# Weight preparation before the plain block: half-size block loads, output weights kept in place, stores on another queue, another order

## The chip, the cores and the metric

The kernel runs on one core of a Trainium2 chip. The metric is the device time of one execution in microseconds. Three executions of the kernel before took 1728.92, 1729.54 and 1729.87 us; their median is 1729.54 us.

## What is computed

Pooled attention (8 batches, 8 heads, 576 tokens, head width 64; keys and values are averaged over groups of 8) gives x of 4608 tokens by 512. Two feed-forward layers follow:

```python
h = (x @ w1) * (x @ w2) @ w3
x = h @ w_out                                  # 4608 x 512
xn = x / sqrt(mean(x * x) + 1e-6) * rms_g
g = xn @ w_gate                                # 512 -> 1536
out = (g * sigmoid(g) * (xn @ w_val)) @ w_out2 # 1536 -> 512
```

The weights come in as float64. The change touches only the weights of the second layer, w_gate, w_val and w_out2.

## The kernel before

The tokens are worked on in 9 blocks of 512. Every fp32 product is made of three matmuls (`mm3`, L86 to L89) of numbers split in a high and a low half (`split`, L82: ScalarE writes the high half, VectorE the low one). The first layer runs for blocks 0 to 8 in turn. The second layer then takes block 0 alone, by plain products (this is "the plain block", `gv` and `o_mm`), and blocks 1 to 8 in pairs, by a scheme with seven products in place of eight (`quad`, `o_part`), for which sums and differences of weight quarters are needed.

**Weight preparation.** `prep` (L807 to L815) is a list of steps that turns float64 weights into split fp32. Its unit is a `Conv` job on a 128x512 piece: `s0` loads it on SyncE's queue (L108) into one of three `raw` buffers, `s1` is one ScalarE and two VectorE instructions (L124 to L128), `s2` two more on VectorE (L133, L141), `s3` whatever comes behind it. `conv_steps(..., 2)` runs them as a pipeline: step k issues the load of job k+2, `s1` of job k, `s2` of job k-1 and `s3` of job k-2.

- `gv_jobs(G, s, kp)` is two jobs; G is 0 to 2, s is 0 for w_gate and 1 for w_val, kp a half of the rows. Behind the second, `sums` forms four more quarters (T1 to T4, L751), splits two tiles of eight quarters (L755, L756) and stores each in two DMAs of 512 KB (L763) to a DRAM scratch, `wdram[s, c, z]`, with c = 2G and 2G+1, where z = 0 holds the quarters T1, T2, B11, B12 and z = 1 holds B21, B22, T3, T4.
- `o2_jobs(g)` is four jobs for four row blocks of w_out2; behind the last, `done` splits them (ScalarE L83, VectorE L84, 128x2048) into two tiles of the pool `r` and stores these to the scratch `odram[g]` (L793, L794).

The order before is: G = 0 (8 jobs), output part 0 (4), G = 1 (8), output part 1 (4), G = 2 (8), output part 2 (4); with the pipeline's two extra steps these are 38 steps. 14 of them run during the first layer's block 7, 5 in the first half of block 8, 4 in its second half, and 15 (`rest`) in the plain block. `Ticker` spreads them: one call after each unit of matmuls, about one step a call.

**Use.** `ring_load(z, n)` (L820 to L829) loads one half of the weights of step n of the second layer from `wdram`, 1024 KB, into one of four buffers of the pool `wB`; steps n = 0 to 11 belong to the plain block. `gv` reads only the quarters B11, B12, B21 and B22 of what was loaded. `o2_load(n)` (L838 to L845) loads the two split tiles of an output part from `odram`, 1024 KB each, into the pool `wC` (four buffers, which hold the first layer's last weights `wph`, `wpl` until block 8 is done). In the plain block the loop over c = 0 to 5 runs 12 matmuls for each `gv` and each `o_mm`, with a call of `tick()` between them, and `o_mm(0, m)` uses output part m // 4 from c = 1 on.

**Queues.** All these loads and stores are issued by SyncE (SP), one behind the other; an issue whose semaphore is not there holds up all that stand behind it. The order on the queue is that of the program as the framework lowers it, which may move an issue past another whose buffer is not free yet. GpSimd (POOL) issues only the accumulating loads of k and v in attention, and computes one small power for each block's norm (L609), between two tiny transfers on SP (L605 and L610).

Of the kernel before, what the change touches and what calls it, by code (L numbers as in the profile page):

```python
# [8 lines left out]
F32 = mybir.dt.float32  # L9
# [11 lines left out]
def kernel(  # L21
# [19 lines left out]
    nc = tc.nc  # L41
# [9 lines left out]
    NB = NT // TB  # L51
    KD = DM // P
    KF1 = F1 // P
# [9 lines left out]
    wC_p = ctx.enter_context(tc.tile_pool(name="wC", bufs=4))  # L63
# [15 lines left out]
    def wtile(pool, nm):  # L79
        return pool.tile([P, 4, 512], F32R, tag="w", name=nm)  # L80
# [464 lines left out]
    for n in range(NW3):  # L545
        g, j = divmod(n, KF1)
# [116 lines left out]
    pipe = Pipe()  # L663
# [49 lines left out]
    NCH = KF2 // 2  # L713
# [8 lines left out]
    }  # L722
    odram = [dram_p.tile([2, P, 4, DM], F32, name=f"od{g}") for g in range(KF2 // 4)]
    ready = set()

    def rtile(nm, dt=F32R):
        return r_p.tile([P, 2048], dt, tag="r", name=nm)

    def gv_jobs(G, s, kp):
        cell = {}  # L730
        w = (w_gate, w_val)[s]

        def quart(z):
            if "f" not in cell:
                cell["f"] = rtile("wf", F32).rearrange("p (j f c) -> p j f c", j=2, f=8)
            f = cell["f"].bitcast(I32)
            return f[:, :, 2 + 2 * z : 4 + 2 * z, :]

        def sums(_):
            f = cell.pop("f")  # L740

            def q(n):
                return f[:, :, FI[n], :]

            for o, x, y in (
                ("T1", "B12", "B11"),
                ("T2", "B22", "T1"),
                ("T3", "B22", "B12"),
                ("T4", "B21", "T2"),
            ):  # L750
                nc.vector.tensor_tensor(out=q(o), in0=q(x), in1=q(y), op=ALU.subtract)  # L751
            for j in range(2):
                c = 2 * G + j
                st = rtile("wst").rearrange("p (f l c) -> p f l c", f=8, l=2)
                nc.scalar.copy(st[:, :, 0, :], f[:, j])  # L755
                nc.vector.tensor_tensor(  # L756
                    out=st[:, :, 1, :],
                    in0=f[:, j],
                    in1=st[:, :, 0, :].bitcast(F32),
                    op=ALU.subtract,  # L760
                )
                for z in range(2):
                    nc.sync.dma_start(  # L763
                        out=wdram[s, c, z][:, :, kp],
                        in_=st[:, 4 * z : 4 * z + 4].bitcast(F32),
                    )
                ready.add((s, c, kp))

        def view(z):
            return z.rearrange("p (j f c) -> p j f c", j=2, f=2)  # L770

        def src(z):
            k0 = (2 * z + kp) * P
            return w[k0 : k0 + P, G * 512 : (G + 1) * 512]

        return [
            Conv(src(0), raw_p, out=lambda: quart(0), view=view),
            Conv(src(1), raw_p, out=lambda: quart(1), view=view, then=sums),
        ]

    def o2_jobs(g):
        cell = {}

        def row(j):
            if j == 0:
                cell["f"] = rtile("of", F32).rearrange("p (j c) -> p j c", j=4)
            return cell["f"].bitcast(I32)[:, j, :]

        def done(_):
            f = cell.pop("f")  # L790
            hi, lo = (rtile(n).rearrange("p (j c) -> p j c", j=4) for n in ("oh", "ol"))
            split(hi, lo, f)
            nc.sync.dma_start(out=odram[g][0], in_=hi.bitcast(F32))  # L793
            nc.sync.dma_start(out=odram[g][1], in_=lo.bitcast(F32))  # L794
            ready.add(g)

        return [
            Conv(
                w_o2[(4 * g + j) * P : (4 * g + j + 1) * P, :],
                raw_p,  # L800
                out=lambda j=j: row(j),
                then=done if j == 3 else None,
            )
            for j in range(4)
        ]

    prep = []  # L807
    for G in range(3):
        part = [gv_jobs(G, s, kp) for s in range(2) for kp in range(2)]
        part = part + [o2_jobs(G)] if G == 0 else part  # L810
        if G == 2:
            part = [o2_jobs(1)] + part + [o2_jobs(2)]
        for p in part:
            prep += p
    prep = conv_steps(prep, 2)  # L815


# [1 line left out]
    ring, ring_n = {}, [0, 0]  # L819

    def ring_load(z, n):
        while ring_n[z] <= min(n, len(SEQ) - 1):
            m = ring_n[z]
            c, s = SEQ[m]
            assert (s, c, 0) in ready and (s, c, 1) in ready
            t = wB_p.tile([P, 4, 512], F32R, tag="w", name=f"wr{z}")
            ring[m, z] = t.rearrange("p f (k l c) -> p f k l c", k=2, l=2)
            nc.sync.dma_start(out=ring[m, z].bitcast(F32), in_=wdram[s, c, z])
            ring_n[z] += 1  # L829

    def wq(n, form, kp):
# [1 line left out]
        t = ring[n, f // 4]  # L833
        return t[:, f % 4, kp, 0, :], t[:, f % 4, kp, 1, :]

    o2r, o2_n = {}, [0]

    def o2_load(n):  # L838
        while o2_n[0] <= min(n, 3 * (1 + NB // 2) - 1):
            g = o2_n[0] % 3  # L840
            assert g in ready
            o2r[o2_n[0]] = [wtile(wC_p, nm) for nm in ("oh", "ol")]
            for l, t in enumerate(o2r[o2_n[0]]):
                nc.sync.dma_start(out=t.bitcast(F32), in_=odram[g][l])
            o2_n[0] += 1  # L845
# [31 lines left out]
    def xn_steps(i):  # L877
        seq = [lambda: (xn_load(i, 0), xn_load(i, 1))]
        return seq + [lambda kk=kk: xn_split(i, kk) for kk in range(KD)]
# [223 lines left out]
    def spread(steps, n):  # L1103
        return steps + [lambda: None] * (n - len(steps))

    pipe.run(NB - 2, range(KF1), ab, y_mm, Ticker(prep[:14], 3 * KF1 - 1))
    xt.pop(NB - 2)
    pipe.run(NB - 1, range(4), ab, y_mm, Ticker(prep[14:19], 12))
    ring_load(0, 1)
    ring_load(1, 1)  # L1110
    pipe.run(NB - 1, range(4, KF1), ab, y_mm, Ticker(prep[19:23] + xn_steps(0), 12))
    xt.pop(NB - 1)
    early, forms = xprep(1)
    rest = prep[23:]
    tick = Ticker(rest + early + forms, 30)
    gv(0, 0)
    gv(1, 0)
    pipe.fin()
    o2_load(0)
    for c in range(NCH):  # L1120
        if c:
            gv(2 * c, 0)
            tick()
            gv(2 * c + 1, 0)
            tick()
            ring_load(0, 2 * c + 2)
            ring_load(1, 2 * c + 2)
            o_mm(0, 2 * c - 2)
            tick()
        for f in range(2):  # L1130
            if pipe.todo:
                pipe.todo.pop(0)()
            gv(2 * c + f, 1)
            tick()
            if c and f == 0:
                o_mm(0, 2 * c - 1)
                tick()
        if c == 0:
            for st in pipe.todo:
                st()  # L1140
        ring_load(0, 2 * c + 3)
        ring_load(1, 2 * c + 3)
        if c == 1:
            o2_load(1)
        elif c == 4:
            o2_load(2)
    tick.flush()
    o_mm(0, 2 * NCH - 2)
    xn.pop(0)
# [62 lines left out]
```

## Time and profile before

| | |
|---|---|
| median of three executions | 1729.54 us |
| the profiled execution | 1729.85 us |
| its span, first to last instruction | 1728.0 us |
| TensorE busy | 1632.6 us (94%), 7252 matmuls |
| VectorE busy | 1050.2 us (61%) |
| ScalarE busy | 643.9 us (37%) |
| GpSimd busy | 59.1 us (3%) |
| mean granted TensorE clock | 0.985 |
| DMA moved | 288.95 MB, mean 167 GB/s |

Busy time of TensorE counts pipelined matmuls, so a stretch can be nearly all busy and yet hold fewer matmuls than it could; the number of matmuls in a stretch, given as (x...), says more. Times in the views are us from the span's start. The plain block lies between about 837 and 985 us.

### The profile page before, as it was taken

What the parts mean: (1) busy time and instruction counts of PE and PEld (TensorE: products, weight loads), DVE (VectorE), ACT (ScalarE), POOL (GpSimd) and SP (SyncE); (2) the same over time, 40 slices, a digit from 0 to 9 for tenths busy, and PEclk for the clock granted to TensorE, in tenths of its full rate; (3) what the DMA queues carried; (4) which work ended last, traced back from release to release, by engine and by line L of the source; (5) the groups of instructions that cost most, each with busy time, mean ns of one, the idle gap of its engine ahead of it and who ended that gap; (6) DMA issues with size and microseconds to landing.
All of it is one profiled execution on the core that took longest, in us unless ns stands there. A gap on an engine that the chain in (4) does not pass through costs nothing.

```text
span 1728.0 us, 19733 instructions
## 1 busy us (share of the span) xinstructions
PE 1632.6 (94%) x7252; PEld 1279.5 (74%) x7252; DVE 1050.2 (61%) x1885; ACT 643.9 (37%) x1568; POOL 59.1 (3%) x50
## 2 busy tenths in 40 slices
PE   6898999999999999999767999999999999999999
PEld 3566677777777777778555778888888888888887
DVE  7874574849494847878484654476255745465344
ACT  3644533333333343434332333243333234233321
POOL 0001000000100000000000000000000000000000
PEclk9999999999999999999888999999999999999999
DMA  9855232322223110588889975466454645455421
GB/s 259 213 149 104 59 70 48 60 68 40 70 38 80 26 52 1 183 292 310 305 288 406 388 280 182 160 231 244 164 202 180 248 169 218 147 196 203 184 99 74
DMA packets 144885, 288.95 MB, mean 167 GB/s; under 512 B 50954, under 2 KB 102154, under 8 KB 124820
## 3 DMA queue, kind: packets, MB, share of 16 engines
q1 hardware_dynamic: 131988, 278.23, 46.4%
q0 software_dynamic: 12800, 9.46, 4.0%
q8 instruction: 57, 0.93, 0.2%
q14 instruction: 40, 0.33, 0.1%
HBM read 237.26 MB, written 50.37 MB: 166 GB/s over the span
## 4 chain that ended last, share of the span: by engine, by line
PE 51%; issue 20%; DVE 9%; DMA 7%; ACT 2%; POOL 1%; SPq 1%; POOLq 0%; ACTq 0%
PE ps L87 9%; PE ps L88 9%; PE ps L89 9%; PE o L89 5%; PE o L88 5%; PE o L87 5%; DVE aT L329 5%; DMA kv<-in_v_dram 4%; PE y L88 2%; PE y L89 2%; PE y L87 2%; DMA wr<-wd 1%; ACT s L301 1%; PE ps L387 1%; DVE f L627 1%
## 5 line engine op out<-in xcount | busy, mean ns | idle before, releaser
L87 PE MATMUL ps<-xf,wr 128*128 128x512 f32 x576 | 227.9, 396 | 1.8 <-DVE f L1010 1.8
L88 PE MATMUL ps<-xf,wr 128*128 128x512 f32 x576 | 227.9, 396 | 0.0
L89 PE MATMUL ps<-xf,wr 128*128 128x512 f32 x576 | 227.8, 395 | 0.0
L87 PE MATMUL o<-oh,hch 128*128 128x512 f32 x384 | 149.4, 389 | 0.0
L88 PE MATMUL o<-ol,hch 128*128 128x512 f32 x384 | 149.4, 389 | 0.0
L89 PE MATMUL o<-oh,hcl 128*128 128x512 f32 x384 | 149.4, 389 | 0.0
L1006 ACT COPY f<-ps 128x512 f32<-128x512 f32 x144 | 84.4, 587 | 169.8 <-PE ps L89 165.2
L329 DVE STREAM_TRANSPOSE aT<-s 32x256 f32<-32x256 f32 x324 | 140.9, 435 | 5.5
L301 ACT ACTIVATE s<-ps,mx 128x72 f32<-128x72 f32 (+1 forms) x320 | 98.0, 322 | 106.3 <-DVE mx L298 106.3
L87 PEld LDWEIGHTS ps<-xf,wr 128*128 128x128 f32 x576 | 108.5, 188 | 27.7 <-DVE f L1010 2.2
L88 PEld LDWEIGHTS ps<-xf,wr 128*128 128x128 f32 x576 | 108.8, 189 | 25.6
L89 PEld LDWEIGHTS ps<-xf,wr 128*128 128x128 f32 x576 | 108.8, 189 | 25.5
L87 PE MATMUL y<-hh,wph 128*128 128x512 f32 x288 | 117.6, 410 | 7.2 <-DVE wpl L84 5.1
L87 PE MATMUL ps<-xh,w2h 128*128 128x512 f32 x288 | 117.9, 409 | 6.2 <-DVE f L627 3.5
L1010 DVE TENSOR_TENSOR f<-y,f 128x512 f32<-128x512 f32 x48 | 33.2, 691 | 148.5 <-PE y L89 148.5
L87 PE MATMUL ps<-xh,w1h 128*128 128x512 f32 x288 | 115.5, 401 | 2.2 <-ACT s L301 2.0
L88 PE MATMUL y<-hl,wph 128*128 128x512 f32 x288 | 114.0, 396 | 1.0 <-DVE hl L84 1.0
L89 PE MATMUL y<-hh,wpl 128*128 128x512 f32 x288 | 113.4, 394 | 0.0
L89 PE MATMUL ps<-xh,w2l 128*128 128x512 f32 x288 | 113.0, 393 | 0.0
L88 PE MATMUL ps<-xl,w2h 128*128 128x512 f32 x288 | 112.8, 392 | 0.0
L88 PE MATMUL ps<-xl,w1h 128*128 128x512 f32 x288 | 112.5, 391 | 0.0
L89 PE MATMUL ps<-xh,w1l 128*128 128x512 f32 x288 | 112.5, 390 | 0.0
(149 smaller groups left out, 3018.8 us busy)
## 6 DMA issues: line engine op xcount, KB each, us to landing
wr<-wd SPq DMA_DIRECT2D x120, 1024.0 KB
wd<-wst SPq DMA_DIRECT2D x48, 512.0 KB
raw<-in_moe_w_dram SPq DMA_DIRECT2D x32, 512.0 KB
oh<-od SPq DMA_DIRECT2D x15, 1024.0 KB
ol<-od SPq DMA_DIRECT2D x15, 1024.0 KB
raw<-in_moe_w_out_dram SPq DMA_DIRECT2D x20, 512.0 KB
ydram<-f SPq DMA_DIRECT2D x36, 256.0 KB
q<-in_q_dram SPq DMA_DIRECT2D x32, 256.0 KB
```

The lines of the kernel that those rows point to most:

```text
L87: nc.tensor.matmul(o, lh, rh, start=first, stop=False, skip_group_check=part)
L88: nc.tensor.matmul(o, lh, rl, start=False, stop=False, skip_group_check=part)
L89: nc.tensor.matmul(o, ll, rh, start=False, stop=last, skip_group_check=part)
L301: nc.scalar.activation(s_t[t][:n, h, :SP], pv[:, j, :], AF.Exp, bias=mx[:, j, :], accum_out=den_t[t][:n, h, :],)
L329: nc.vector.transpose(aT[32 * kb : 32 * kb + 32, :, s0 + 32 * i : s0 + 32 * i + 32], s_t[t][32 * i : 32 * i + 32, :, 32 * kb : 32 * kb + 32],)
L387: nc.tensor.matmul(ps[j * D : (j + 1) * D, :n], st8["vp", b][:, h * D : (h + 1) * D], st8["aT", b][:SP, h, c0 : c0 + n], start=True, stop= ...
L627: nc.vector.tensor_tensor(out=hf, in0=ps, in1=a0.pop((i, m)), op=ALU.mult)
L1006: nc.scalar.copy(t, bank)
L1010: nc.vector.tensor_tensor(out=t, in0=bank, in1=t, op=ALU.add)
```

## The change

- In the plain block `ring_load` loads only two of the four quarters of each half, 512 KB in place of 1024 KB (the two that `gv` reads). The 24 loads of steps 0 to 11 are concerned; later steps load all.
- `o2_jobs` takes its two tiles from the pool `wC` and writes the split weights straight into the tiles that `o_mm` reads. The first three `o2_load` calls (six loads of 1024 KB) are gone; the stores to `odram` remain, for the later pairs of blocks.
- The stores to `wdram` (48 of 512 KB) and to `odram` (6 of 1024 KB) are issued on GpSimd's queue in place of SyncE's.
- The order of jobs is now G = 0, G = 1, then the first job pair of G = 2, output part 0, two pairs of G = 2, output part 1, the last pair of G = 2, output part 2. 13, 4 and 4 steps run in block 7 and in the halves of block 8, 17 in the plain block. The load of block 0's activations for the plain block (`xn_load`, the first of `xn_steps(0)`) moves from the second half of block 8 to the end of its first half.

```diff
--- before.py
+++ after.py
@@ -722,6 +722,7 @@
     }
     odram = [dram_p.tile([2, P, 4, DM], F32, name=f"od{g}") for g in range(KF2 // 4)]
     ready = set()
+    o2r = {}
 
     def rtile(nm, dt=F32R):
         return r_p.tile([P, 2048], dt, tag="r", name=nm)
@@ -760,7 +761,7 @@
                     op=ALU.subtract,
                 )
                 for z in range(2):
-                    nc.sync.dma_start(
+                    nc.gpsimd.dma_start(
                         out=wdram[s, c, z][:, :, kp],
                         in_=st[:, 4 * z : 4 * z + 4].bitcast(F32),
                     )
@@ -788,11 +789,10 @@
 
         def done(_):
             f = cell.pop("f")
-            hi, lo = (rtile(n).rearrange("p (j c) -> p j c", j=4) for n in ("oh", "ol"))
+            hi, lo = o2r[g] = [wtile(wC_p, nm) for nm in ("oh", "ol")]
             split(hi, lo, f)
-            nc.sync.dma_start(out=odram[g][0], in_=hi.bitcast(F32))
-            nc.sync.dma_start(out=odram[g][1], in_=lo.bitcast(F32))
-            ready.add(g)
+            nc.gpsimd.dma_start(out=odram[g][0], in_=hi.bitcast(F32))
+            nc.gpsimd.dma_start(out=odram[g][1], in_=lo.bitcast(F32))
 
         return [
             Conv(
@@ -806,12 +806,12 @@
 
     prep = []
     for G in range(3):
-        part = [gv_jobs(G, s, kp) for s in range(2) for kp in range(2)]
-        part = part + [o2_jobs(G)] if G == 0 else part
-        if G == 2:
-            part = [o2_jobs(1)] + part + [o2_jobs(2)]
-        for p in part:
-            prep += p
+        for s in range(2):
+            for kp in range(2):
+                if (G, kp) == (2, 1):
+                    prep += o2_jobs(s)
+                prep += gv_jobs(G, s, kp)
+    prep += o2_jobs(2)
     prep = conv_steps(prep, 2)
 
 
@@ -825,7 +825,10 @@
             assert (s, c, 0) in ready and (s, c, 1) in ready
             t = wB_p.tile([P, 4, 512], F32R, tag="w", name=f"wr{z}")
             ring[m, z] = t.rearrange("p f (k l c) -> p f k l c", k=2, l=2)
-            nc.sync.dma_start(out=ring[m, z].bitcast(F32), in_=wdram[s, c, z])
+            fs = slice(0, 4)
+            if m < 2 * NCH:
+                fs = slice(2 - 2 * z, 4 - 2 * z)
+            nc.sync.dma_start(out=ring[m, z][:, fs].bitcast(F32), in_=wdram[s, c, z][:, fs])
             ring_n[z] += 1
 
     def wq(n, form, kp):
@@ -833,12 +836,11 @@
         t = ring[n, f // 4]
         return t[:, f % 4, kp, 0, :], t[:, f % 4, kp, 1, :]
 
-    o2r, o2_n = {}, [0]
+    o2_n = [3]
 
     def o2_load(n):
         while o2_n[0] <= min(n, 3 * (1 + NB // 2) - 1):
             g = o2_n[0] % 3
-            assert g in ready
             o2r[o2_n[0]] = [wtile(wC_p, nm) for nm in ("oh", "ol")]
             for l, t in enumerate(o2r[o2_n[0]]):
                 nc.sync.dma_start(out=t.bitcast(F32), in_=odram[g][l])
@@ -1103,20 +1105,19 @@
     def spread(steps, n):
         return steps + [lambda: None] * (n - len(steps))
 
-    pipe.run(NB - 2, range(KF1), ab, y_mm, Ticker(prep[:14], 3 * KF1 - 1))
+    pipe.run(NB - 2, range(KF1), ab, y_mm, Ticker(prep[:13], 3 * KF1 - 1))
     xt.pop(NB - 2)
-    pipe.run(NB - 1, range(4), ab, y_mm, Ticker(prep[14:19], 12))
+    pipe.run(NB - 1, range(4), ab, y_mm, Ticker(prep[13:17] + xn_steps(0)[:1], 12))
     ring_load(0, 1)
     ring_load(1, 1)
-    pipe.run(NB - 1, range(4, KF1), ab, y_mm, Ticker(prep[19:23] + xn_steps(0), 12))
+    pipe.run(NB - 1, range(4, KF1), ab, y_mm, Ticker(prep[17:21] + xn_steps(0)[1:], 12))
     xt.pop(NB - 1)
     early, forms = xprep(1)
-    rest = prep[23:]
+    rest = prep[21:]
     tick = Ticker(rest + early + forms, 30)
     gv(0, 0)
     gv(1, 0)
     pipe.fin()
-    o2_load(0)
     for c in range(NCH):
         if c:
             gv(2 * c, 0)
@@ -1140,10 +1141,6 @@
                 st()
         ring_load(0, 2 * c + 3)
         ring_load(1, 2 * c + 3)
-        if c == 1:
-            o2_load(1)
-        elif c == 4:
-            o2_load(2)
     tick.flush()
     o_mm(0, 2 * NCH - 2)
     xn.pop(0)
```

## Rows read from the trace of the kernel before

**Rows 1.** The page: busy tenths of TensorE and its clock in 40 slices of 43.2 us.
```profile
PE   6898999999999999999767999999999999999999
...
PEclk9999999999999999999888999999999999999999
```

**Rows 2.** Windows: stretch, length, busy us and count of each engine, clock, DMA share, GB/s.
```profile
760.00:780.00 20.00, 20.00 (x90) 16.57 (x89) 17.00 (x29) 11.00 (x17) 0.00 (x0) 1.00 0.83 305
740.00:840.00 100.00, 95.68 (x414) 76.80 (x413) 71.33 (x122) 40.35 (x60) 1.68 (x1) 1.00 0.93 329
840.00:940.00 100.00, 63.93 (x241) 50.01 (x240) 61.23 (x108) 34.29 (x47) 4.10 (x2) 0.81 0.87 320
940.00:980.00 40.00, 34.74 (x148) 27.47 (x148) 28.46 (x34) 11.61 (x15) 0.00 (x0) 1.00 0.97 381
```

**Rows 3.** What TensorE waited for from 837 to 985 us: total, times, longest.
```profile
PE ps L87 <- DMA wr<-wd: 30.6, 7, 15.0
PE ps L599 <- ACT f L591: 10.4, 1, 10.4
```

**Rows 4.** TensorE's timeline around the longest wait (start, length, [idle before, releaser]).
```profile
910.04 0.80 PE L87 MATMUL ps<-xnh,wr 128*128 128x512 f32 x1 [15.02 <-DMA wr<-wd]
910.63 0.63 PE L88 MATMUL ps<-xnl,wr 128*128 128x512 f32 x1
911.06 0.63 PE L89 MATMUL ps<-xnh,wr 128*128 128x512 f32 x1
```

**Rows 5.** SyncE's queue in the same time: start and length of each issue.
```profile
894.50 1.21 SPq L763 DMA_DIRECT2D wd<-wst  x2
899.55 0.33 SPq L610 DMA_DIRECT2D rdram<-ss  x1
899.98 1.20 SPq L763 DMA_DIRECT2D wd<-wst  x2
...
902.35 1.68 SPq L828 DMA_DIRECT2D wr<-wd  x2
...
905.79 11.05 SPq L763 DMA_DIRECT2D wd<-wst  x4
916.93 1.92 SPq L828 DMA_DIRECT2D wr<-wd  x1
```

**Rows 6.** What SyncE's queue waited for from 837 to 945 us.
```profile
SPq L610 <- POOL ss L609: 10.0, 2, 6.2
SPq L828 <- PE ps L89: 9.5, 5, 3.7
```

**Rows 7.** DMA queues of the page: packets, MB, share of 16 engines' time.
```profile
q1 hardware_dynamic: 131988, 278.23, 46.4%
q0 software_dynamic: 12800, 9.46, 4.0%
```

**Rows 8.** VectorE's groups from 690 to 1000 us, shapes kept apart: count, busy, mean ns.
```profile
L756 DVE TENSOR_TENSOR wst<-wf,wst 128x1024 fp32r<-128x1024 f32 x24 | 28.9, 1219 | 5.5 <-ACT wst L755 5.5
L133 DVE SCALAR_TENSOR_TENSOR raw<-raw 128x512 int32<-128x512 int32 x33 | 22.6, 687 | 4.7 <-ACT raw L124 4.7
L751 DVE TENSOR_TENSOR wf<-wf 128x256 f32<-128x256 f32 x48 | 18.4, 418 | 0.2
L128 DVE TENSOR_SCALAR f<-f 128x512 int32<-128x512 int32 x36 | 15.2, 423 | 0.5
L84 DVE TENSOR_TENSOR ol<-of,oh 128x2048 fp32r<-128x2048 f32 x3 | 6.9, 2291 | 2.5 <-ACT oh L83 2.5
```

**Rows 9.** GpSimd: its loads of k (issue to landing 6.9 us), its issues, two powers.
```profile
kv<-in_k_dram POOLq DMA_DIRECT2D x16, 288.0 KB, 6.9
...
L209 POOL DMA_DIRECT2D kv<-in_k_dram x16 | 19.8, 1235 | 345.2 <-DVE f L582 266.0 <-DMA kv<-in_k_dram 37.1 <-DVE f L125 34.8
...
648.66 1.01 POOL L609 TENSOR_TENSOR ss<-ss,mhalf 128x4 f32<-128x4 f32 x1 [76.42 <-DVE ss L606]
731.27 7.40 POOL L609 TENSOR_TENSOR ss<-ss,mhalf 128x4 f32<-128x4 f32 x1 [81.61 <-DVE ss L606]
```

## The prediction, made before the changed kernel ran

> **What bounds the kernel now.** I read the page's 40 slices first. TensorE sits at 9 in every slice from the fifth on, except slices 20 to 22 (counted from 1: 821 to 950 us) with 7, 6 and 7, where the granted clock also falls to 8 [rows 1]. That is where the plain block begins, and where the rest of the weight preparation runs. Then I counted matmuls in windows. A full stretch holds 90 in 20 us, one every 0.222 us. From 840 to 940 us there are 241, worth 53.6 us, so 46.4 us are lost; from 940 to 980 us 148, worth 32.9, so 7.1 are lost [rows 2]. Those 53.5 us are nearly all that this change can win; before 840 us the shortfall in the count is 8 us in 100 us, and a few missing records can make part of it.
>
> What TensorE waits for there: 30.6 us in seven waits for the block loads, and 10.4 us in one wait for the sums of squares of block 8 [rows 3]. After each long wait the matmuls come 0.43 us apart in place of 0.22 for eight to twelve of them, the lower of the two clock levels; with four such restarts that is some 8 us [rows 4]. 30.6 + 10.4 + 8 = 49 of the 53.5 us are named.
>
> Why are the loads late? The one that ends the 15 us wait was issued at 902.35 and landed by 910.04. On SyncE's queue stand ahead of it two pairs of stores and the rdram store of the norm, which itself waits for GpSimd; from 894.50 on the queue does little but wait. Right behind, four stores take 11.05 us to issue, and the next block load comes only at 916.93 [rows 5]. So two things make the loads late: a queue held up by stores, and transfers that are themselves slow because the DMA engines are 87% busy, 97% in the next stretch [rows 2]. VectorE is busy 61.2 us of the hundred: not the bound, but near.
>
> **The change part by part.**
>
> *Half loads.* 24 loads lose 0.52 MB each, 12.6 MB. In the window the engines move 320 GB/s at a share of 0.87, so 368 GB/s when busy: 1.4 us of DMA time for each half, 34 us in all. Of the 24, four are issued before 840 us, twelve between 840 and 940, eight after. *First output loads.* Six of 1.05 MB fall away, 2.85 us each, 17 us in all; two lie before 840 us, two in the hundred, two behind.
>
> *Order.* Output part 0 moves from block 7 into the plain block: its two stores (5.7 us of DMA) and two more raw loads (2.9 us) come into the hundred. DMA time there: 87 - 12 x 1.4 - 2 x 2.85 + 8.6 = 73 us. VectorE: the plain block's list holds the first part of 15 jobs in place of 13 (2 x 0.42 us each) and the second part of 16 in place of 14 (2 x 0.69 us each), three output splits in place of two (2.3 us), and three weight groups in place of four (a group is four of 0.42 and two of 1.22, 4.1 us) [rows 8]: +1.7 + 2.8 + 2.3 - 4.1 = +2.7 us, so 64 us. TensorE's own work is 54 us and does not change.
>
> *Stores on GpSimd's queue.* SyncE loses 54 issues and their waits for VectorE; GpSimd gains them. In the trace a GpSimd issue of 288 KB takes 1.24 us and lands in 6.9 us [rows 9]; a store here has 512 pieces of 1 KB against 288, so I take 1.2 x 512/288 = 2.1 us. Fifty-four of them are 113 us on an engine idle from 690 to 950 us except for the powers. What waits behind them is the power of block 8 and SyncE's rdram store behind that: up to four stores, 8 us, at most twice; SyncE already waits 10.0 us there [rows 6]. I charge 2 us. As for the transfer, the trace has only accumulating DMAs on queue 0: 4.0% of 16 x 1728 us for 9.46 MB is 117 us per MB and engine, against 46 on queue 1 [rows 7]. Bounds for a 512 KB store are thus 1.5 us of all engines (as queue 1) and 3.8 us (as queue 0). I take the lower end, since an accumulation has a second read that a plain store has not; the upper end goes into the range.
>
> *Output weights in place.* The split waits for `wph`, `wpl`, which TensorE has left before the plain block's loop; the third part waits for `o_mm(0, 3)`, four calls ahead of its split. Nothing is late by that. But part 0 is now split in the third call and first read after the fourth, only one `gv` (12 x 0.222 = 2.7 us) later; ScalarE's half and then VectorE's (2.3 us [rows 8]) do not fit fully: between 0 and 5 us, I charge 2, since TensorE stands a few units behind VectorE there. *Activations earlier.* `xn_load` is earlier by half a block; it takes two of three raw buffers while four jobs want them. Both signs are possible, below 3 us, taken as nothing: VectorE has half a block (4 x 36 matmuls, 32 us) for what the wait delays.
>
> **The sum.** In 840 to 940 us the largest floor left is DMA's 73 us, then VectorE's 64, TensorE's 54. No engine runs gaplessly through such a chain, and SyncE's own waits for freed buffers (9.5 us) and for the power remain [rows 6]; I put the stretch at 78, a gain of 22 us. In 940 to 980 us DMA falls from 39 us by 8 x 1.4 + 2 x 2.85 = 17, TensorE becomes the bound, and 5 of 7 us come back. Before 840 us 11 us of DMA time in front of the plain block go: 4 us, half of the shortfall there. 22 + 5 + 4 - 2 - 2 = 27 us. The profiled execution took 1729.85 (span 1728.0 and 1.85 around it), so 1702.9; the median of the runs is 0.3 lower: 1702.5 us. What is late next should be VectorE's part of the preparation.
>
> **The rivals.**
>
> *VectorE takes over.* If conversion, splits and the block's own products alternate rather than overlap, VectorE's 64 us become the pace with TensorE's waits between them, and the stretch falls only to 90: a gain of 10 and 5 behind it, less 4, so about 11 us, 1719. For it: VectorE has 61 of 100 us even now. Against: no wait of TensorE's on VectorE is among the large ones [rows 3].
>
> *The bytes don't matter.* If the loads are late through their order alone (freed buffers, the power, the landing of stores before them), a half load changes little, and what the free queue wins the later output part loses: within 3 us of 1729.5. Against: 0.87 and 0.97 DMA share.
>
> *The stores choke on GpSimd's queue: slower.* A power of 128x4 took 7.40 us at 731 us, where VectorE ran without a gap, and 1.01 at 648 us, where it did not [rows 9]. If each store is held up like that, the three weight groups of G = 2 that are stored in the plain block need 12 x 7.4 = 89 us from the fifth call on, and the load of step 9 comes at the twentieth, 15 x 2.7 = 41 us later: 48 us late, less the 27 won, so about 1750. It decides from the point where a store costs over (41 + 27)/12 = 5.7 us. Against: the issues beside a busy VectorE in attention took 1.2 us on the mean of 16. The Trainium skill speaks for this rival (SBUF — State Buffer, "SBUF: two separate sides"): a DMA issued from GpSimd cannot write its descriptors while VectorE runs an instruction in a two-port mode, and should go to another queue. Of the conversion only the tensor_scalar instructions are such candidates here (0.42 us for what takes 0.69 in other forms [rows 8]), two a job; by that rule a store waits for one of them at a time, and no run so far shows a store on that queue.
>
> **How the numbers follow.** Forecast 0.63 (gain of 14 to 46 us), VectorE takes over 0.19, bytes don't matter 0.07, stores choke 0.11. About 0.2%, 3.5 us, is what a measurement of this kernel can tell from no change. Faster: 0.63 + 0.19 = 0.82; same 0.07; slower 0.11. The low end is VectorE's floor reached and all the rest won: 100 - 64 + 7 + 4 = 47 us, 1683. The high end takes in the second rival and stops ahead of the third: 1724, a gain of 6.
>
> **What would show it.** Right: in the new trace the waits for the block loads fall from 30.6 us to below 10, the DMA share in the plain block falls below 0.85, block loads are issued within 2 us of the buffer coming free, the clock stays at its upper level through slices 20 to 22, and GpSimd's stores take about 2 us. Wrong: issues of 4 us and more on GpSimd with block loads waiting for them; TensorE waiting for the output split in place of a load; VectorE above 0.9 through the block; or waits for block loads that remain with a DMA share of half.

## The result, and the profile after

The changed kernel takes 1714.8 us (median of four runs, 1713.8 to 1718.2) beside 1729.7 for the kernel before: a ratio of 0.9917, with a 95% interval of 0.9899 to 0.9934. The gain is 14.9 us; the forecast was 27, the range 6 to 46. The profiled execution took 1713.81 us, its span is 1711.9.

The page of the changed kernel, first TensorE's 40 slices with the granted clock, then the DMA queues (packets, MB, share of 16 engines):

```profile
PE   7898999999999999999978999999999999999999
...
PEclk9999999999999999999998999999999999999999
...
DMA packets 125588, 270.07 MB, mean 158 GB/s; under 512 B 50858, under 2 KB 77482, under 8 KB 109364
...
q1 hardware_dynamic: 104916, 227.89, 39.2%
q0 software_dynamic: 20576, 40.92, 9.3%
```

Three weak slices have become two, and one slice is left at a lower clock [rows 1]. Queue 1 moves 50.3 MB less: 31.5 MB of stores went to queue 0, and 18.9 MB are not moved at all (24 half loads of 0.52 MB, six output loads of 1.05).

The windows of rows 2 for the changed kernel (length, then busy time and count of PE, PEld, DVE, ACT, POOL; then the granted clock, DMA share, GB/s):

```profile
740.00:840.00 100.00, 90.62 (x379) 71.06 (x378) 73.08 (x129) 39.08 (x60) 21.42 (x27) 0.98 0.79 264
840.00:940.00 100.00, 83.92 (x319) 63.79 (x318) 65.36 (x115) 36.42 (x50) 13.93 (x19) 0.90 0.72 259
940.00:980.00 40.00, 35.78 (x154) 28.29 (x154) 28.88 (x35) 13.10 (x18) 0.65 (x2) 1.00 0.92 348
```

Read against [rows 2]: in the plain block's hundred the matmuls rise from 241 to 319 and the DMA share falls from 0.87 to 0.72 (forecast 0.73). But in the hundred before it the matmuls fall, from 414 to 379. Something was lost where the forecast had a small gain.

TensorE's waits in the plain block, 844 to 985 us (total, times, longest):

```profile
PE y L87 <- ACT hh L83: 7.9, 3, 3.9
PE ps L87 <- DMA wr<-wd: 5.3, 4, 2.0
PE ps L599 <- ACT f L591: 2.7, 1, 2.7
PE ps L87 <- DVE f L907: 2.4, 1, 2.4
```

The block loads cost 5.3 us in place of 30.6, the sums of squares 2.7 in place of 10.4 [rows 3]. On SyncE's queue no weight store stands ahead of the loads any more, though the norm's rdram store still does; the first view is its timeline, the second what it waited for from 838 to 945 us:

```profile
896.37 0.32 SPq L610 DMA_DIRECT2D rdram<-ss  x1
896.79 1.49 SPq L831 DMA_DIRECT2D wr<-wd  x1
...
912.10 1.92 SPq L831 DMA_DIRECT2D wr<-wd  x3
```

```profile
SPq L831 <- PE ps L89: 24.9, 6, 15.1
SPq L610 <- POOL ss L609: 9.8, 2, 6.9
```

The queue now reaches the loads early and waits for their buffers, 24.9 us in place of 9.5, while the wait for the power stays at 9.8 beside 10.0 [rows 5, 6].

Now the loss. TensorE's waits in blocks 7 and 8, 696 to 838 us:

```profile
PE y L87 <- ACT hh L83: 5.1, 5, 2.1
PE y L88 <- DVE hl L84: 4.6, 8, 2.3
```

The same view of the kernel before, 698 to 828 us:

```profile
PE y L87 <- ACT hh L83: 1.7, 1, 1.7
...
PE y L88 <- DVE hl L84: 0.2, 1, 0.2
```

`hh` and `hl` are the rounded halves of the first layer's result, which the products with `wph`, `wpl` read. TensorE now waits for them in thirteen places instead of two, 9.7 us in all. What holds ScalarE, which makes `hh`, is in its own waits in the changed kernel, 696 to 838 us:

```profile
ACT raw L124 <- DMA raw<-in_moe_w_out_dram: 15.5, 3, 7.8
ACT xnh L874 <- DVE raw L871: 14.1, 4, 7.2
ACT raw L124 <- DMA raw<-in_moe_w_val_dram: 11.3, 8, 3.5
ACT raw L124 <- DMA raw<-in_moe_w_gate_dram: 7.2, 5, 4.3
```

34.0 us of waiting (15.5 + 11.3 + 7.2) for weights that have not come: a conversion (L124) waits at the head of ScalarE, and the cast that TensorE needs stands behind it. The sum alone does not tell the two kernels apart, for in the kernel before, 698 to 828 us, ScalarE waits 28.0 us for the same weights, and TensorE hardly feels it:

```profile
ACT raw L124 <- DMA raw<-in_moe_w_out_dram: 19.4, 8, 8.0
ACT raw L124 <- DMA raw<-in_moe_w_val_dram: 4.5, 5, 1.6
ACT raw L124 <- DMA raw<-in_moe_w_gate_dram: 4.1, 2, 2.3
```

What counts is what stands behind the waiting instruction. ScalarE's timeline of the changed kernel shows a cast that does (its input was ready at 793.9 us; TensorE, which still had other products, lost 0.4 us by it):

```profile
798.55 0.66 ACT L124 ACTIVATE raw<-raw 128x512 int32<-128x512 uint32 x1 [7.75 <-DMA raw<-in_moe_w_out_dram]
799.11 0.60 ACT L83 CAST hh<-f 128x512 fp32r<-128x512 f32 x1
```

It is not only ScalarE. TensorE's two longest waits in these blocks, 2.26 and 2.08 us, end behind VectorE's first instruction on the activations (L871), which waits 5.46 us for the broadcast of the norm and, the second time, 3.54 us for the activations themselves. With the 0.44 us right behind the second these are 4.8 of the 9.7 us. The first of the two:

```profile
809.99 0.69 DVE L871 TENSOR_TENSOR raw<-raw,f 128x512 f32<-128x512 f32 x1 [5.46 <-DMA f<-rdram]
810.60 0.68 DVE L84 TENSOR_TENSOR hl<-f,hh 128x512 fp32r<-128x512 f32 x1
811.34 0.50 PE L88 MATMUL y<-hl,wph 128*128 128x512 f32 x1 [2.26 <-DVE hl L84]
```

To compare all kernels below I use marks in the trace that move with the work: the starts of TensorE's first matmul of block 7, of its last product with `w1` in block 8 (12 products with `w2` and 24 with `wph`, `wpl` of that block are still to come), and of its first pair matmul (`ps<-xf,wr`), and the span's end.

| profiled execution, us | start of block 7 | blocks 7 and 8 | from there to the first pair | pairs to the end |
|---|---|---|---|---|
| before | 698.3 | 129.5 | 159.8 | 740.4 |
| after | 696.0 | 141.5 | 137.8 | 736.6 |
| difference | -2.3 | +12.0 | -22.0 | -3.8 |

So the plain block won what was forecast, and 12 us were given back ahead of it. The start of block 7 is no more than a mark: over all versions below it lies between 695.2 and 701.1 us, though no edit is about the work ahead of it, so differences of 2 or 3 us there say nothing.

### The profile page after: what moved, and what is told of

The parts are those of the page before. It is cut to its first block, busy times and chain, and to the rows that moved or that the text cites. A ratio compares the mean times of both kernels' runs of the same rounds, so it can differ in the third digit from the quotient of the medians.

```text
span 1711.9 us, 19765 instructions
## 1 busy us (share of the span) xinstructions
PE 1636.2 (96%) x7252; PEld 1278.1 (75%) x7252; DVE 1050.0 (61%) x1885; ACT 643.9 (38%) x1568; POOL 91.1 (5%) x104
## 2 busy tenths in 40 slices
DMA packets 125588, 270.07 MB, mean 158 GB/s; under 512 B 50858, under 2 KB 77482, under 8 KB 109364
## 3 DMA queue, kind: packets, MB, share of 16 engines
q0 software_dynamic: 20576, 40.92, 9.3%
## 4 chain that ended last, share of the span: by engine, by line
PE 43%; DMA 6%; DVE 4%; issue 1%; ACT 1%; POOL 0%; SPq 0%; DVEq 0%; ACTq 0%; POOLq 0%
PE ps L88 8%; PE ps L89 8%; PE ps L87 8%; PE o L89 5%; PE o L87 5%; PE o L88 5%; PE y L89 1%; PE y L88 1%; PE y L87 1%; DMA raw<-in_moe_w_out_dram 1%; DMA xq<-ydram 1%; DMA raw<-in_moe_w_gate_dram 1%; DMA raw<-in_moe_w_val_dram 1%; DVE wst L757 1%; DMA ydram<-f 1%
```

## The experiments

The forecast's own theory is that half loads and the free queue win the plain block. For the loss in blocks 7 and 8 there were these candidates: the earlier load of activations holds two of three raw buffers; the new order of jobs is worse; stores on GpSimd disturb the hardware (DMA, ports); or the instructions of ScalarE, VectorE and TensorE are placed in another order. The time after each ratio is a median; blocks 7 and 8 are read from the profiled execution, as in the table.

### One part alone on the kernel before

**Only the stores on GpSimd's queue** (54 issues):

```diff
-                    nc.sync.dma_start(
+                    nc.gpsimd.dma_start(
                         out=wdram[s, c, z][:, :, kp],
...
-            nc.sync.dma_start(out=odram[g][0], in_=hi.bitcast(F32))
-            nc.sync.dma_start(out=odram[g][1], in_=lo.bitcast(F32))
+            nc.gpsimd.dma_start(out=odram[g][0], in_=hi.bitcast(F32))
+            nc.gpsimd.dma_start(out=odram[g][1], in_=lo.bitcast(F32))
```

> The kernel before, with the 54 stores issued by GpSimd and nothing else changed. The changed kernel won about 22 us between the end of block 8 and the first pair of blocks, and lost about 12 us in blocks 7 and 8. Theory A (the loss comes from the earlier load of the activations, which holds two of three raw buffers): the stores alone cost nothing in blocks 7 and 8 and free SyncE's queue, 5 to 10 us faster than before, 1720 to 1725 us. Theory B (the loss comes from the stores on GpSimd's queue, which slow VectorE or the raw loads): blocks 7 and 8 take 8 to 12 us longer than before, the whole 1728 to 1736 us.

1736.4 us, ratio 1.0035 (1.0014 to 1.0056). Blocks 7 and 8 take 145.7 us, 16.2 longer; from there to the first pair 150.2, 9.6 shorter. This one edit carries the whole loss. TensorE's waits, 698 to 1010 us, and ScalarE's for raw weights, 698 to 848 us:

```profile
PE y L87 <- ACT hh L83: 13.7, 8, 5.4
PE ps L87 <- DMA wr<-wd: 13.5, 9, 4.2
```

```profile
ACT raw L124 <- DMA raw<-in_moe_w_out_dram: 21.0, 7, 5.1
ACT raw L124 <- DMA raw<-in_moe_w_gate_dram: 17.0, 4, 7.8
ACT raw L124 <- DMA raw<-in_moe_w_val_dram: 10.9, 6, 3.8
```

**Only the half loads:**

```diff
-            nc.sync.dma_start(out=ring[m, z].bitcast(F32), in_=wdram[s, c, z])
+            fs = slice(0, 4)
+            if m < 2 * NCH:
+                fs = slice(2 - 2 * z, 4 - 2 * z)
+            nc.sync.dma_start(out=ring[m, z][:, fs].bitcast(F32), in_=wdram[s, c, z][:, fs])
```

> The kernel before, with the half loads in the plain block and nothing else changed. If bytes bound the plain block: 34 us of DMA time less, a third to a half of it on the path, 1714 to 1722 us. If the loads are late through their order on the queue alone: within 3 us of before, 1727 to 1732 us. Blocks 7 and 8 as before (129.5 us together) by either theory.

1705.6 us, ratio 0.9861 (0.9830 to 0.9892): 24 us, more than the whole change won and more than was expected. Blocks 7 and 8 stay at 129.9; the plain block gives 16.8 (143.0). TensorE's waits, 698 to 990 us, then the plain block's hundred:

```profile
PE ps L87 <- DMA wr<-wd: 20.7, 5, 11.1
```

```profile
840.00:940.00 100.00, 73.74 (x283) 57.55 (x282) 64.04 (x109) 34.12 (x47) 2.49 (x2) 0.85 0.84 286
```

The bytes matter, but the loads are still late by 20.7 us, with the stores ahead of them on the queue.

### The candidates for the loss, on the kernel after

**The activations' load back in the second half of block 8:**

```diff
-    pipe.run(NB - 1, range(4), ab, y_mm, Ticker(prep[13:17] + xn_steps(0)[:1], 12))
+    pipe.run(NB - 1, range(4), ab, y_mm, Ticker(prep[13:17], 12))
...
-    pipe.run(NB - 1, range(4, KF1), ab, y_mm, Ticker(prep[17:21] + xn_steps(0)[1:], 12))
+    pipe.run(NB - 1, range(4, KF1), ab, y_mm, Ticker(prep[17:21] + xn_steps(0), 12))
```

> The changed kernel, with the activations' load and its four splits all in the second half of block 8 again. Theory A: blocks 7 and 8 come back to about 131 us from 141.5, the plain block starts as late as before; 1703 to 1708 us. Theories B (stores) and C (the new order of the jobs loads VectorE at the wrong time): no change, 1713 to 1718 us.

1715.7 us, ratio 0.9910 (0.9876 to 0.9945). Blocks 7 and 8 take 138.1, 3.4 less, and the stretch behind gives the same back (141.2 for 137.8). So the earlier load decides where some of the time is lost (the 4.8 us above), but the total does not come back with it: it is not the cause.

**The activations in buffers of their own**, so that they hold none of the raw ones:

```diff
-        r = raw_p.tile([P, 1024], I32, tag="raw", name="raw").bitcast(F32)
+        r = r_p.tile([P, 1024], F32, tag="xq", name="xq", bufs=2)
```

> The changed kernel, with the activations loaded into the two buffers xq, which are free at that time, in place of two of the three raw buffers; order as changed. Theory A: raw loads are not held up any more, blocks 7 and 8 take 130 to 134 us, the whole 1701 to 1707 us. Theories B and C: 1713 to 1718 us.

1710.3 us, ratio 0.9885 (0.9856 to 0.9915); blocks 7 and 8 at 139.8. The held buffers are worth some 4.5 us of the total (the two intervals overlap), but only 1.7 of the 12.0 in question.

**All stores back on SyncE**, the rest of the change kept:

```diff
-                    nc.gpsimd.dma_start(
+                    nc.sync.dma_start(
                         out=wdram[s, c, z][:, :, kp],
...
-            nc.gpsimd.dma_start(out=odram[g][0], in_=hi.bitcast(F32))
-            nc.gpsimd.dma_start(out=odram[g][1], in_=lo.bitcast(F32))
+            nc.sync.dma_start(out=odram[g][0], in_=hi.bitcast(F32))
+            nc.sync.dma_start(out=odram[g][1], in_=lo.bitcast(F32))
```

> The changed kernel with all 54 stores back on SyncE's queue; half loads, output weights in place and the new order stay. Stores alone on GpSimd cost 16 us in blocks 7 and 8 and won 10 us behind them (run b_pool). If that carries over: blocks 7 and 8 come back to 130 to 134 us from 141.5, the stretch from the end of block 8 to the first pair grows from 138 to 142 to 148; the whole 1704 to 1712 us. Rival: the new order or the output weights in place make blocks 7 and 8 long; then they stay at 138 to 142 and the whole is 1715 to 1722 us.

1699.8 us, ratio 0.9820 (0.9794 to 0.9845), 15 us below the changed kernel and below the range expected. Blocks 7 and 8 take 126.0 and TensorE waits for nothing in them. So the new order of jobs is not the cause either. In the plain block the loads are late again, but for no more than the new waits of the other version (137.1 beside 137.8); TensorE's waits, 701 to 985 us:

```profile
PE ps L87 <- DMA wr<-wd: 22.2, 4, 13.5
```

**The stores divided between the queues**: the weight stores of G = 0 and 1, made in blocks 7 and 8, on SyncE; those of G = 2 and the output's on GpSimd:

```diff
-                    nc.gpsimd.dma_start(
+                    (nc.sync, nc.gpsimd)[G // 2].dma_start(
```

> The changed kernel with the weight stores of G = 0 and 1 on SyncE's queue again and those of G = 2 and of the output parts on GpSimd's. If the stores cost in blocks 7 and 8 and win in the plain block: 130 to 134 us for the two blocks and 136 to 141 behind them, 1700 to 1707 us. Rival (order or output weights make the two blocks long): 1712 to 1718 us.

1696.3 us, ratio 0.9795 (0.9762 to 0.9828): the lowest median of all, below both kernels. Blocks 7 and 8 stay at the 126.0 of all stores on SyncE: in the traces of the two versions the orders of ScalarE, VectorE and TensorE are the same up to the mark of block 8. The next stretch falls to 134.1. Its lead over the version with all stores on SyncE, 3.5 us, is smaller than the spread of its own runs (1691.9 to 1700.0), so that lead is likely rather than settled. TensorE's waits, 701 to 985 us:

```profile
PE y L87 <- ACT hh L83: 7.7, 2, 4.1
PE ps L87 <- DMA wr<-wd: 5.9, 4, 2.5
```

### Order of instructions, or hardware?

With the stores on another queue, the built program itself differs: the framework places the instructions of ScalarE and VectorE in another order, though the source of their work is the same. In the traces of the kernel before and of its version with stores on GpSimd, ScalarE's first 20 instructions from the start of block 7 and VectorE's first 42 are alike, and then they part; so they do between the changed kernel and its version with all stores on SyncE (20 and 41). TensorE's order does not change in either pair, through its 555 matmuls up to the mark of block 8. ScalarE's list in block 7, from the last cast ahead of the parting:

```
before:              L83 hh; L755 x2; L624; L124 x2; L83 hh; L755 x2; L624; L83 hh; L124 x2; ...
stores on GpSimd:    L83 hh; L124; L755 x2; L124; L624; L83 hh; L124; L755 x2; L624; L124; L83 hh; L124; ...
```

With the stores on GpSimd a conversion, which needs a raw load, stands directly ahead of 9 of the 14 casts of `hh` in blocks 7 and 8; in the kernel before it does of 5. To tell this from a disturbance by the stores themselves, order and queue must be varied apart.

**First attempt: both versions in program order.** The three calls that make blocks 7 and 8 were built with ScalarE, VectorE and TensorE kept as written (activations in their own buffers, as above), once with the stores on SyncE, once on GpSimd:

```diff
+    ms = tc.manual_schedule(engines={mybir.EngineType.Activation, mybir.EngineType.DVE, mybir.EngineType.PE})
+    ms.__enter__()
     pipe.run(NB - 2, range(KF1), ab, y_mm, Ticker(prep[:14], 3 * KF1 - 1))
...
     pipe.run(NB - 1, range(4, KF1), ab, y_mm, Ticker(prep[19:23] + xn_steps(0), 12))
+    ms.__exit__(None, None, None)
```

> The kernel before, with ScalarE, VectorE and TensorE held to the program's own order in blocks 7 and 8 (and the activations loaded into the buffers xq, without which that order would block itself). It is one half of a pair with b_pool_ms: the same order of instructions with the stores on either queue. Alone: blocks 7 and 8 in 128 to 140 us; the whole 1722 to 1740 us.

> As b_ms, with the 54 stores on GpSimd's queue. Theory D (the stores cost nothing by themselves; once they leave SyncE's queue, the framework, which places instructions by its own estimate, puts conversions ahead of the casts that TensorE waits for): with the order held, blocks 7 and 8 are within 3 us of those of b_ms. Theory E (the hardware: stores that run beside the raw loads make these land later, in whatever order): blocks 7 and 8 are 8 to 14 us longer than in b_ms.

1774.2 us on SyncE (1.0255, 1.0221 to 1.0289) and 1750.7 on GpSimd (1.0111, 1.0077 to 1.0146). Blocks 7 and 8 take 165.0 and 163.4: with one order the queue makes no loss. But program order is itself 35 us slower there, outside the expected range, for another reason: on SyncE, ScalarE waits 53.1 us for VectorE's part of the same work, and so little for raw loads that the suspected wait is hardly in this pair:

```profile
ACT hh L83 <- DVE f L627: 53.1, 13, 12.9
...
ACT raw L124 <- DMA raw<-in_moe_w_gate_dram: 2.4, 2, 1.4
```

It speaks against the hardware, but is a weak test.

**Second attempt: one version held to the other's order.** The order of the three engines' instructions in these blocks was read from one built kernel, and written into another as a chain of plain order edges (no semaphores):

```diff
+    for name, steps in ORDER.items():
+        engine = getattr(mybir.EngineType, name)
+        traced = [i for i in nc.cur_bb.bb.instructions if i.engine == engine]
...
+                tc.add_manual_dep(
+                    traced[at],
+                    prev.name,
+                    mybir.DependencyInfo(
+                        mybir.DependencyClass.NoSync, mybir.DependencyReason.DATA
+                    ),
+                    reason="order",
+                )
```

The kernel before with its stores on GpSimd, held to the order that the kernel before has:

> As b_pool (54 stores on GpSimd's queue, nothing else changed), with the instructions of TensorE, VectorE and ScalarE held to the order that they have in the kernel before. Theory D (order): blocks 7 and 8 back to 127 to 134 us (before 129.5, b_pool 145.7), and the 10 us won behind them stay; 1716 to 1724 us. Theory E (the stores' traffic beside the raw loads): blocks 7 and 8 at 140 to 147 us, the whole 1730 to 1738 us.

The kernel before, its stores on SyncE, held to the order that stores on GpSimd bring:

> The kernel before, stores on SyncE's queue, with the instructions of TensorE, VectorE and ScalarE held to the order that they have in b_pool. Theory D: blocks 7 and 8 take 140 to 148 us though no store has moved, the whole 1736 to 1750 us. Theory E: 127 to 134 us and 1727 to 1733 us.

The changed kernel, all stores on GpSimd, held to the order of its version with all stores on SyncE:

> The changed kernel, all 54 stores on GpSimd's queue as it has them, with the instructions of the three engines held to the order that they have in a_sp. Theory D: blocks 7 and 8 at 125 to 130 us (changed kernel 141.5, a_sp 126.0), the whole 1694 to 1702 us. Theory E: 138 to 143 us and 1711 to 1718 us.

| | time, us | ratio (95%) | blocks 7 and 8, us |
|---|---|---|---|
| before, own order | 1729.7 | 1 | 129.5 |
| before, other order | 1743.9 | 1.0083 (1.0051 to 1.0114) | 137.7 (140.4 for the same work) |
| stores on GpSimd, own order | 1736.4 | 1.0035 (1.0014 to 1.0056) | 145.7 |
| stores on GpSimd, before's order | 1725.0 | 0.9972 (0.9953 to 0.9991) | 132.5 |
| changed, own order | 1714.8 | 0.9917 (0.9899 to 0.9934) | 141.5 |
| changed, order of all stores on SyncE | 1701.7 | 0.9832 (0.9794 to 0.9870) | 126.0 |

How far the order was held can be read from the traces. In the two held versions with stores on GpSimd all three engines run, up to the mark of block 8, exactly what they run in the kernel whose order they were given. In the kernel before with the other order ScalarE (82 instructions) and VectorE (177) do, but TensorE does not: after 171 matmuls it leaves the order of both kernels, and so this run differs from the kernel before in three engines. One place of many, where the version with stores on GpSimd runs products with `wph` between the two lines:

```profile
833.55 0.39 PE L89 MATMUL ps<-xh,w2l 128*128 128x512 f32 x1
833.78 0.39 PE L87 MATMUL ps<-xh,w1h 128*128 128x512 f32 x1
```

Up to the mark it has made 168 of the 180 products with `wph`, `wpl` that every other version has; the 12 missing ones are 2.7 us, hence the second figure in its row.

On the changed kernel the order is the whole loss: the same stores on the same queue, and blocks 7 and 8 go from 141.5 to 126.0. The windows over those blocks, first as changed, then held (columns as above):

```profile
696.00:838.00 142.00, 132.29 (x560) 104.78 (x559) 105.92 (x188) 57.45 (x88) 30.32 (x38) 0.99 0.76 257
```

```profile
700.00:826.00 126.00, 126.00 (x556) 103.83 (x557) 104.91 (x188) 57.28 (x87) 29.56 (x38) 1.00 0.84 287
```

As changed, TensorE is idle for 9.7 us and takes 6.3 more for the same matmuls; held, it never stops, while VectorE, ScalarE and GpSimd do the same work. ScalarE's waits for raw weights fall with it, from 34.0 us to 11.4 (1.3 for w_gate beside the two shown), 699 to 826 us:

```profile
ACT raw L124 <- DMA raw<-in_moe_w_out_dram: 7.0, 3, 6.3
...
ACT raw L124 <- DMA raw<-in_moe_w_val_dram: 3.1, 3, 1.6
```

On the kernel before with its stores on GpSimd, the order is 13.2 of the 16.2 us (145.7 - 132.5). The 3.0 us that remain beside the kernel before (132.5 - 129.5) are no price of the queue that could be told: that execution began block 7 at 695.2 us, 3.1 earlier, and both reach the mark of block 8 together (827.7 and 827.8). The reverse, the bad order with the stores on SyncE, costs 8.2 us by the mark, less than the 10 to 18 expected, 10.9 for the same work, and 14.2 in the whole time, but TensorE's order is mixed into it.

Measured to TensorE's last product with `wph`, `wpl`, where the first layer is done in all of them, the four read 143.3 (SyncE) and 144.2 us (GpSimd) in the order of the kernel before, 163.9 (SyncE) and 164.2 (GpSimd) in the other: some 20 us by the order, of which 2.7 are 12 more products of the plain block that stand ahead of that mark in the other order, and less than 1 by the queue. In the whole time GpSimd's queue wins, 4.7 us under the one order (1729.7 - 1725.0) and 7.5 under the other (1743.9 - 1736.4).

So the loss belongs to the order in which ScalarE and VectorE work: in both kernels it goes when the good order is held, with every store on GpSimd. Which of the two engines' lists matters more is not separated, since they were held together, and the lists of SyncE and GpSimd were not held. Why the framework places the work otherwise is not in a trace.

### Are the half loads the plain block's gain?

**The changed kernel with stores on SyncE and full loads**, that is, new order, output weights in place and earlier activations alone:

```diff
-            if m < 2 * NCH:
-                fs = slice(2 - 2 * z, 4 - 2 * z)
```

> The changed kernel with all stores on SyncE's queue and full loads in the plain block: what is left is the new order, the output weights in place and the earlier activations. The half loads alone won 24 us (b_half). If the parts add up, this is 1720 to 1727 us, 3 to 10 us faster than before. If the half loads were worth that much only because the output loads stood in the same queue, this is 1706 to 1714 us.

1712.9 us, ratio 0.9909 (0.9877 to 0.9941). These parts alone are worth 17 us, as the second of the two expectations has it, and the plain block still waits 26.7 us for its loads (TensorE's waits, 830 to 990 us):

```profile
PE ps L87 <- DMA wr<-wd: 26.7, 5, 15.1
```

The half loads add 13.1 to that (1712.9 - 1699.8), though alone they give 24: 17 and 24 make 30 together. Both shorten the plain block, and the pairs of blocks behind it take 737.0 us with the half loads alone and 737.1 with the other parts alone, as with both (736.9). Blocks 7 and 8 take 126.0 us with full loads too. Moving only the plain block's stores to GpSimd takes that stretch from 137.1 to 134.1.

## Why the prediction was right, and where it was off

The direction and the range held, and of the likeliest case's mechanism most parts are found in the trace. The size was off, 15 us for 27, mainly by one term. That the range held in spite of it is owed to its width: a loss of this kind was in none of the rivals.

**The plain block** was to win 22 and 5 us, less two charges of 2: 23. By the marks it won 22.0, and the pairs behind it another 3.8, which no step had; the stores alone do not bring them (740.4 us there, as before), the half loads alone do (737.0), and so do the other parts alone (737.1). Why is open. The fixed window from 940 to 980 us can't be compared, since the work in it is now some 12 us further on (the first pair comes at 975.3 us for 987.6), and its forecast DMA time of 22 us (39 - 17) reads 0.92 of 40 there.

**The sum's terms, one by one.** The DMA share came out as worked out (0.72 of the hundred for 0.73), VectorE's busy time too (65.4 us for 64). The block loads' waits fell to 5.3 us, below the 10 named. SyncE no longer comes late to the loads but stands waiting for buffers, six times; that was to be "issued within 2 us", and for these six it fits. The clock is only half right: slice 22 (899 to 942 us) still reads 8, and the hundred has 0.90; two of the three waits for `hh`, 3.9 and 2.9 of the 7.9 us, end in that slice. The two charges were not what was feared: SyncE's wait for the power stayed (9.8 us). What is late next is not VectorE's part of the preparation by itself but a raw load, and what stands behind its conversion. In the longest of these waits VectorE had finished its part at 896.7 us, and ScalarE's cast stood behind a conversion:

```profile
898.05 0.68 ACT L124 ACTIVATE raw<-raw 128x512 int32<-128x512 uint32 x1 [7.15 <-DMA raw<-in_moe_w_out_dram]
898.64 0.60 ACT L83 CAST hh<-f 128x512 fp32r<-128x512 f32 x1
899.29 0.79 PE L87 MATMUL y<-oh,hh 128*128 128x512 f32 x1 [3.92 <-ACT hh L83]
```

In the second, both engines stood at a conversion for the same load (2.56 and 2.84 us, to 914.5 us).

**A price that was too high.** I took 2.1 us for a store's issue on GpSimd. GpSimd's groups of instructions give it, and its timeline the power of block 7, at the place of the one of 7.40 us in [rows 9]:

```profile
L764 POOL DMA_DIRECT2D wd<-wst x48 | 36.1, 809 | 156.2 <-DVE wst L757 87.1 <-PE ps L600 69.0
```

```profile
725.52 1.40 POOL L609 TENSOR_TENSOR ss<-ss,mhalf 128x4 f32<-128x4 f32 x1 [6.11 <-DVE ss L606]
```

0.81 us an issue on the mean, where SyncE's of the same stores have a median of 0.65 in the kernel before, and a power of 1.40. The rival in which stores choke on that queue was for the point of 5.7 us; it did not happen. The rule of the Trainium skill that spoke for it (SBUF — State Buffer, "SBUF: two separate sides") leaves no visible mark in these traces: the stores land 5.7 us after issue, and VectorE's conversions beside them keep their times, here in blocks 7 and 8 of the kernel before with stores on GpSimd (421 and 424 ns without them):

```profile
L125 DVE TENSOR_SCALAR f<-raw 128x512 f32<-128x512 f32 x23 | 9.9, 434 | 3.5 <-DMA raw<-in_moe_w_out_dram 3.5
L128 DVE TENSOR_SCALAR f<-f 128x512 int32<-128x512 int32 x23 | 9.7, 422 | 0.3
```

**The step that failed** is "Before 840 us 11 us of DMA time in front of the plain block go: 4 us". It measured a loss: 12.0 us in the blocks, 9.7 by the time at which they end. Behind it stands a statement that the text never made: that a store on another queue leaves every other instruction where it was. I priced the stores as issues and transfers, at 2.1 us each; the price that came was in ScalarE's and VectorE's order. With the order held, the version with the stores where the change puts them takes 1701.7 us, beside the forecast of 1702.5; but that is the sum's terms coming out with more than one size shifted, and not a proof of each. Then the blocks are 3.5 us shorter than before (126.0 beside 129.5), near the 4 of the term, but not by its half loads: with full loads they are 126.0 as well, and the half loads alone leave them at 129.9.

**The earlier activations** were "both signs, below 3 us, taken as nothing". Moved back, they make no difference in the total (1715.7 beside 1714.8); given buffers of their own they are worth some 4.5. The bound was a little narrow. That VectorE has time enough for what the wait delays did not hold in the order as built: VectorE stands still for 5.46 us, and the first layer's `hl` behind it comes late. In the good order VectorE waits 5.3 us at the same place, and TensorE loses nothing.

**The rival "the bytes don't matter"** fell with the half loads alone, 24 us. Of **"VectorE takes over"**, which gave nearly the measured time (1719), little is to be seen: TensorE's largest wait on VectorE in the plain block is 2.4 us, and VectorE's 65.4 us were no pace. A rival can have the right time by the wrong way.

## What to carry to other kernels

A DMA's queue is also an input to whatever orders the instructions: after moving one, compare the order on every other engine before and after, and look for an instruction that waits for a load ahead of one that TensorE needs. The sum of an engine's waits does not tell: 28.0 us of them were nearly harmless in one order, 34.0 went with a loss of 12 us in another. Moving only the stores that stand ahead of a late load left the order in the blocks before as it was; that version has the lowest median here, by a lead that isn't settled. Where two parts of a change shorten the same stretch, price them together: 24 and 17 us alone made 30.

## What the runs showed of the hardware that was not expected

The same stores go in larger packets from GpSimd's queue. Queue 0 has 7776 packets more than before (20576 - 12800) [rows 7]: that is 48 stores of 512 KB in pieces of 4 KB (6144), six of 1 MB in pieces of 8 KB (768), and 864 small ones (54 x 16), for rows of 1 KB in DRAM; the page's packets under 2 KB are 77482, and 102058 in the same kernel with all stores on SyncE, which moves the same bytes. It makes them no cheaper: (9.3% x 16 x 1711.9 - 4.0% x 16 x 1728.0) / 31.46 MB = 45.8 us per MB and engine, as on queue 1 (46). The lower bound taken for the transfer was the right one.

An issue of 512 KB on GpSimd costs 0.81 us, less than the 1.24 of an accumulating load of 288 KB there [rows 9]. The four stores that took SyncE 11.05 us to issue [rows 5] are no measure of that queue: of the 48 there the median is 0.65 us, and one of these four took 7.72, in a stretch (905.79 to 916.84 us) with a DMA share of 1.00. In the changed kernel with all stores on SyncE, the median is 0.63 and the longest 1.60.
